# Plain column order for the moving operand of the first twelve feed-forward tasks, and a strided sigmoid read

## The chip, the cores and the metric

The kernel runs on one core of one Trainium2 chip. The metric is device microseconds (us) of one execution, lower is better. The engines are TensorE (PE, with its weight loads as PEld), VectorE (DVE), ScalarE (ACT), GpSimd (POOL) and SyncE (SP). SP and POOL issue nearly all the DMAs here.

## The reference, cut to what matters

Per batch and head a recurrent state of 48 by 48 is decayed, updated and read at each of 768 steps. The 3072 output rows of width 384 then go through a feed-forward network (FFN). With `x` the reshaped output of the recurrence:

```python
y[:, :, t] = einsum('bhd,bhde->bhe', rt, state + cur)
state = wt[:, :, :, None] * state + einsum('bhd,bhe->bhde', kt, vt)
h = x @ w_in                                  # 3072x384 by 384x2048
g = h * (1.0 / (1.0 + np.exp(-1.702 * h)))
out = g @ w_out                               # 2048x384
```

## The kernel before, in words

The 3072 tokens are cut into 24 chunks of 128, and the chunks into six groups of four. `chunk` (L232) computes one chunk of the recurrence in steps on TensorE, VectorE and ScalarE, and leaves it as a high and a low part in fp32r in the tile `x` of its group (128 partitions, 512 token columns). The last twelve chunks (`CROSS`, L75) keep their heads in swapped halves; this touches no line of the change.

The FFN has 96 tasks: six groups by 16 slices of 128 hidden columns. A task has three parts.

- `first_product` (L433) fills the PSUM bank `ph` (two buffers) by nine matmuls of 128 by 512, three terms (high by high, high by low, low by high) for each of three slices of the contraction: L440, L441, L442.
- `gelu` (L445) runs the sigmoid form of gelu twice from `ph` on ScalarE, into `gh` (fp32r, L451) and `gf` (fp32, L452), and VectorE takes the difference as `gl` (L453).
- `second_product` (L456) adds nine matmuls into the three PSUM banks `po`: L466, L467, L468.

The moving operand of each of these matmuls is read through `halves` (L425): column 0, column 256, column 1, column 257 and so on, so two columns that follow each other in the stream lie 1,024 bytes apart. The result is written in memory order (`by_twos`, L429, only gives the output the same shape). Each product thus permutes its columns once. After two products the tokens lie four apart, and `store` (L561) puts them right: its activation L567 reads `po` with a step of four elements (16 bytes) and writes in order.

The weights come as 64-bit integers, and `convert` (L187) turns each of twelve pieces of 128 by 1024 into two fp32r tiles (`pair`). Its six long instructions are L195 and L196 on ScalarE, L198 and L201 on VectorE, then L204 (ScalarE) and L206 (VectorE). The views `l` and `h` (L192) are every second 32-bit word, so L195 (reads and writes `l`), L196 (reads `h`), L198 (reads `h` and `l`, writes `h`) and L201 (reads `h`) step 8 bytes from element to element. L204 and L206 read and write in order.

The order of all work on every engine is written out by hand. Up to task 31 it is the string `RAMP` (L60): `a` is a step of a chunk, `l` a load, `w` a step of a weight conversion, `f` a fetch, `k` a run of bf16 matmuls without use that keeps TensorE busy (L481), and `g`, `h`, `y` with a number are the first product, the gelu and the second product of that task. Tasks 0 to 11 lie where the weights are still being converted. From task 32 on nearly all FFN matmuls run in halves of 64 rows (`on_rows`, L489, matmul L492), two at a time; the last task runs on full rows again. The branch behind L698 (a slower path for extreme inputs) is not entered.

Of the kernel before, what the change touches and what calls it, by code (L numbers as in the profile page):

```python
# [13 lines left out]
AF = mybir.ActivationFunctionType  # L14
# [12 lines left out]
C = P  # L27
# [3 lines left out]
NF = DFF // P  # L31
NM = DM // P
# [8 lines left out]
W_SCALE = 2.0 ** 8  # L41
# [34 lines left out]
WP = NF * DM // NL  # L76
SPLIT = range(FIRST, len(TASKS) - 1)
PHASE = 8
SYNC = mybir.DependencyInfo(mybir.DependencyClass.Sync, mybir.DependencyReason.DATA)
assert sum(CHUNKS) == NT  # L80

# [2 lines left out]
def rwkv_ffn_kernel(ctx: ExitStack, tc, wkr, vp, vrk, ub, w_in, w_out, masks, vt, uc, out):  # L84
    nc = tc.nc
    V, A, G, T = nc.vector, nc.scalar, nc.gpsimd, nc.tensor
# [82 lines left out]
    def fetch(i):  # L169

        s, which = divmod(i, 2)
        n = SL // NL
        st = staged[i] = wt.tile([P, n, 2 * WP // n], I32, tag=f"w{i}", name=f"raw{i}")
        src = (w_in, w_out)[which][s * n : (s + 1) * n].bitcast(I32)
        if which == 0:
            if s == 0:
                nc.sync.dma_start(st[TOP:], src[:, 0 : P - TOP].rearrange("n p w -> p n w"))
            else:
                rows = w_in.bitcast(I32).rearrange("s p w -> (s p) w")[s * n * P - TOP : (s + 1) * n * P - TOP]
                nc.sync.dma_start(st, rows.rearrange("(n p) w -> p n w", p=P))  # L180
            yield
            nc.sync.dma_start(st[0:TOP], src[:, P - TOP :].rearrange("n p w -> p n w"))
        else:
            nc.sync.dma_start(st, src.rearrange("n p w -> p n w"))
        yield
# [23 lines left out]
    def weight(which, f, m):  # L209

        s, n = divmod(f * NM + m, WP // P)
        return (pairs[2 * s + which][:, t, n * P : (n + 1) * P] for t in range(2))

    def split(hi, lo, f):
        A.copy(hi, f)
        V.tensor_tensor(lo, f, hi.bitcast(F32), op=ALU.subtract)  # L216
# [196 lines left out]
    def fill_x(x, c0, c1, cross=False):  # L413

        for m in range(NM):
            for i, dst in enumerate((R2, 0)):
                j = TOP * (2 * m + i + 1)
                G.dma_start(  # L418
                    x[dst : dst + TOP, :, m ^ 2 * (cross and i == 0), c0:c1].bitcast(F32),
                    x[j : j + TOP, :, NM ^ 2 * (cross and j >= HB), c0:c1].bitcast(F32),  # L420
                )

    xs, po, parts, measures, tiled, steady = {}, {}, {}, {}, [], []

    def halves(x):  # L425

        return x.rearrange("p (a b) -> p b a", a=2)

    def by_twos(x):  # L429

        return x.rearrange("p (b a) -> p b a", a=2)

    def first_product(j, task):  # L433
        i, c0, c1, f = task
        cs = slice(c0 * C, c1 * C)
        ph = ps_h.tile([P, WIDE], F32, tag="ph", name="ph")[:, 0 : (c1 - c0) * C]
        x = xs.get((i, 0), xs[i])
        for c in range(NM):
            h_, l_ = weight(0, f, c)
            T.matmul(by_twos(ph), h_, halves(x[:, 0, c, cs]), start=c == 0, stop=False)  # L440
            T.matmul(by_twos(ph), h_, halves(x[:, 1, c, cs]), start=False, stop=False)  # L441
            T.matmul(by_twos(ph), l_, halves(x[:, 0, c, cs]), start=False, stop=c == NM - 1)  # L442
        parts[j] = ph

    def gelu(j, task):  # L445
        i, c0, c1, f = task
        ph, n = parts[j], (c1 - c0) * C
        gf = mo.tile([P, WIDE], F32, tag="gf", name="gf")[:, 0:n]
        gh = mo.tile([P, WIDE], F32R, tag="gh", name="gh", bufs=LAG + 1)[:, 0:n]
        gl = mo.tile([P, WIDE], F32R, tag="gl", name="gl", bufs=LAG + 1)[:, 0:n]  # L450
        A.activation(gh, ph, AF.Gelu_apprx_sigmoid, scale=1.0 / W_SCALE)  # L451
        A.activation(gf, ph, AF.Gelu_apprx_sigmoid, scale=1.0 / W_SCALE)  # L452
        V.tensor_tensor(gl, gf, gh.bitcast(F32), op=ALU.subtract)  # L453
        parts[j] = gh, gl

    def second_product(j, task):  # L456
        i, c0, c1, f = task
        gh, gl = parts.pop(j)
        first = i not in po
        if first:  # L460
            po[i] = [ps_o.tile([P, WIDE], F32, tag=f"po{m}", name=f"po{m}") for m in range(NM)]
        for m in range(NM):
            h_, l_ = weight(1, f, m)
            o = by_twos(po[i][m][:, c0 * C : c1 * C])

            T.matmul(o, h_, halves(gh), start=first, stop=False, skip_group_check=True)  # L466
            T.matmul(o, l_, halves(gh), start=False, stop=False, skip_group_check=True)  # L467
            T.matmul(o, h_, halves(gl), start=False, stop=f == NF - 1, skip_group_check=True)  # L468

    idle = []  # L470

# [17 lines left out]
    def on_rows(half, bank, out, w, x, start, stop, done):  # L489
# [4 lines left out]
        if before:  # L494
            tc.add_manual_dep(mm.ins, before, SYNC, reason="the bank's other row tile is done")
        if done:
            nop = nc.sync.nop()  # L497
            tc.add_manual_dep(nop.ins, mm.ins.name, SYNC, reason="a row tile is done with a bank")
            relay[bank] = nop.ins.name
# [39 lines left out]
    def rows_of(j):  # L539
# [11 lines left out]
        for k in range(2 * n):  # L551
            for items in (top, bottom):
                if k < len(items) and items[k]:
                    next(items[k], None)
            if k == PHASE and j in SPLIT:
                yield
# [19 lines left out]
    def new_x(i):  # L576

        return mo.tile([P, 2, NP, WIDE], F32R, tag="x", name="x")
# [119 lines left out]
    with tc.If(n < full):  # L698
        with tc.tile_pool(name="wp", bufs=2) as wp:
            for i in range(2 * NL):  # L700
                for part in (fetch(i), convert(i, wp, True)):
                    for _ in part:
                        pass
        with tc.tile_pool(name="gp", bufs=1) as gp, tc.tile_pool(name="ob", bufs=2) as ob, tc.For_i(0, B, 1) as b:
            pools["late"] = ob
            xg = [new_x(i) for i in range(2)]
            for p in range(NP):
                vr = gp.tile([R2, S], F32, tag="vr", name="vr")
                V.memset(vr[0:TOP], 0.0)
                nc.sync.dma_start(vr[TOP:R2], vt[bass.ds(b, 1), p].rearrange("o r s -> (o r) s"))  # L710
                uu = gp.tile([R2, D], F32, tag="uu", name="uu")
                V.memset(uu[0:TOP], 0.0)
                nc.sync.dma_start(uu[TOP:R2], uc[p])
                ya = gp.tile([R2, S], F32, tag="ya", name="ya")
                for d in range(D):
                    rows = []
                    for i, c0 in enumerate((1 + p * CW, 1 + NP * CW + p * C, 1 + NP * CW + NP * C + p * C)):
                        x = gp.tile([R2, CB, C], F32, tag=f"row{i}", name=f"row{i}", bufs=2)
                        for h, n in enumerate((HB, D)):
                            src = wkr[bass.ds(b * CB, CB), h * D + d, c0 : c0 + C]  # L720
                            nc.sync.dma_start(x[h * HB : h * HB + n], src.unsqueeze(0).broadcast_to([n, CB, C]))
                        rows.append(x.rearrange("r c s -> r (c s)"))
                    w_, k_, r_ = rows
                    kv = gp.tile([R2, S], F32, tag="kv", name="kv", bufs=2)
                    V.tensor_tensor(kv, k_, vr, op=ALU.mult)
                    st = gp.tile([R2, S + 1], F32, tag="st", name="st", bufs=2)
                    V.memset(st[:, 0:1], 0.0)
                    V.tensor_tensor_scan(st[:, 1:], w_, kv, 0.0, op0=ALU.mult, op1=ALU.add)
                    V.scalar_tensor_tensor(kv, kv, uu[:, d : d + 1], st[:, 0:S], op0=ALU.mult, op1=ALU.add)
                    if d == 0:  # L730
                        V.tensor_tensor(ya, kv, r_, op=ALU.mult)
                    else:
                        V.tensor_tensor(kv, kv, r_, op=ALU.mult)
                        V.tensor_tensor(ya, ya, kv, op=ALU.add)
                for half in range(2):
                    x = xg[half]
                    split(x[0:R2, 0, p, 0:384], x[0:R2, 1, p, 0:384], ya[:, half * 384 : half * 384 + 384])
                    if p == NM:
                        fill_x(x, 0, 384)
            for half in range(2):  # L740
                xs[half] = xg[half]
                for f in range(NF):
                    task = half, 0, 3, f
                    first_product(f, task)
                    gelu(f, task)
                    second_product(f, task)
                store(half, b * S + half * 384, 384)


# [52 lines left out]
```

## Time and profile before

| what | value |
|---|---|
| median of 3 runs | 517.76 us (517.01 to 518.64) |
| the profiled execution | 517.63 us |
| span of its profile | 515.9 us |
| TensorE busy | 495.0 us, 96% of the span |
| VectorE busy | 295.5 us, 57% |
| ScalarE busy | 289.8 us, 56% |
| mean granted TensorE clock | 0.993 |

The span runs from the first to the last recorded instruction; 1.7 us of the execution's time lie around it. A matmul's busy time includes its pipeline, so matmuls that follow each other without a gap overlap in the records, and the distance from start to start is what one costs. The shares over the whole span hide that the first 160 us have other limits than the rest.

### The profile page before, as it was taken

Reading aid. Unit: us, or ns where it says so; the run is one execution under the profiler, and the core shown is the slowest. Engines: PE = TensorE matmul, PEld = TensorE weight load, DVE = VectorE, ACT = ScalarE, POOL = GpSimd, SP = SyncE. Lnnn points to the kernel's source line nnn. Section 1 sums busy time; section 2 is a strip of 40 time slices with the busy share of each in tenths; the row PEclk is TensorE's granted clock in tenths of the full one; section 3 lists DMA queues with packets and bytes.
Section 4 is the critical chain, followed back from the end, with each engine's and each line's share of the span. In section 5 each row is a group of like instructions: output and inputs, shape, how many; then the busy total and the mean of one; then the engine's idle time right before and its main releaser. Section 6 shows DMA issues by size and latency. Waiting matters only on the chain.

```text
span 515.9 us, 11452 instructions
## 1 busy us (share of the span) xinstructions
PE 495.0 (96%) x4539; PEld 417.4 (81%) x4539; DVE 295.5 (57%) x451; ACT 289.8 (56%) x619; POOL 95.8 (19%) x200
## 2 busy tenths in 40 slices
PE   7999988999998999999999999999999999999994
PEld 4766776888886888878888888898888888888873
DVE  7999999999968312645555554564565422211210
ACT  4988989977864443355455475455365342422322
POOL 2002000000200010048401649301660002210000
PEclk9999999999999999989999999999999999999998
DMA  8998920124463210025210435110531001150001
GB/s 270 302 407 232 352 96 1 63 88 148 134 209 96 82 31 0 1 87 141 67 48 12 114 95 159 42 47 6 120 109 47 1 1 32 44 143 1 1 1 68
DMA packets 19470, 50.30 MB, mean 98 GB/s; under 512 B 4544, under 2 KB 8320, under 8 KB 19408
## 3 DMA queue, kind: packets, MB, share of 16 engines
q1 hardware_dynamic: 11664, 31.24, 18.4%
q0 software_dynamic: 7344, 17.72, 13.2%
q8 instruction: 38, 0.62, 0.5%
q10 hardware_dynamic: 400, 0.53, 0.3%
q14 instruction: 24, 0.20, 0.1%
HBM read 40.82 MB, written 4.72 MB: 88 GB/s over the span
## 4 chain that ended last, share of the span: by engine, by line
PE 68%; DVE 1%; DMA 1%; ACT 0%; SPq 0%; issue 0%; ACTq 0%
PE po L492 26%; PE ph L492 24%; PE ps_s L352 3%; PE ps_c L370 2%; PE po L468 2%; PE po L466 2%; PE ph L440 2%; PE po L467 2%; PE ph L441 2%; PE ph L442 2%; PE ps_c L364 1%; PE ps_u L325 1%; DMA rk_t<-in_vrk 1%; PE ps_t L294 0%; PE ps_y L392 0%; PE ps_y L400 0%
## 5 line engine op out<-in xcount | busy, mean ns | idle before, releaser
L492 PE MATMUL ph<-x,pair 64*128 64x512 f32 x1134 | 186.1, 377 | 0.0
L453 DVE TENSOR_TENSOR gl<-gf,gh 128x512 fp32r<-128x512 f32 x96 | 66.3, 691 | 187.1 <-ACT gf L452 187.0
L492 PE MATMUL po<-gh,pair 64*128 64x512 f32 x768 | 159.0, 388 | 0.2 <-SPq L497 0.2
L492 PEld LDWEIGHTS ph<-x,pair 64*128 64x128 f32 x1134 | 144.0, 187 | 14.1
L451 ACT ACTIVATE gh<-ph 128x512 fp32r<-128x512 f32 x96 | 57.5, 599 | 160.2 <-PE ph L492 137.1
L492 PEld LDWEIGHTS po<-gh,pair 64*128 64x128 f32 x768 | 96.2, 188 | 10.9 <-issue 1.1
L492 PE MATMUL po<-gl,pair 64*128 64x512 f32 x384 | 99.8, 379 | 0.0
L418 POOL DMA_DIRECT2D x<-x x36 | 18.3, 514 | 255.2 <-DVE x L216 214.0
L314 ACT ACTIVATE am<-ident,s 128x128 f32<-128x128 f32 x192 | 58.8, 397 | 2.5 <-issue 1.5
L452 ACT ACTIVATE gf<-ph 128x512 f32<-128x512 f32 x96 | 57.1, 595 | 0.0
L157 POOL DMA_DIRECT2D wkr_t<-in_wkr x108 | 53.9, 506 | 11.4 <-DVE kq L266 6.2
L492 PEld LDWEIGHTS po<-gl,pair 64*128 64x128 f32 x384 | 50.5, 188 | 5.0
L440 PE MATMUL ph<-x,pair 128*128 128x512 f32 x99 | 39.0, 393 | 3.7 <-ACT gf L452 2.8
L468 PE MATMUL po<-gl,pair 128*128 128x512 f32 x96 | 36.8, 383 | 3.4 <-DVE gl L453 3.4
L442 PE MATMUL ph<-x,pair 128*128 128x512 f32 x99 | 37.6, 380 | 0.0
L441 PE MATMUL ph<-x,pair 128*128 128x512 f32 x99 | 37.5, 379 | 0.0
L466 PE MATMUL po<-gh,pair 128*128 128x512 f32 x96 | 37.3, 389 | 0.0
L467 PE MATMUL po<-gh,pair 128*128 128x512 f32 x96 | 36.4, 380 | 0.0
L221 ACT ACTIVATE junk<-lp 112x1032 bf16<-112x1032 f32 x24 | 25.9, 1077 | 12.0 <-DVE lp L251 11.9
L245 DVE TENSOR_TENSOR_SCAN lp<-wkr_t,d1r 112x516 f32<-112x516 f32 x24 | 29.5, 1228 | 1.3 <-POOL ident masks.py:199 0.9
L251 DVE TENSOR_TENSOR_SCAN lp<-wkr_t,d1f 112x516 f32<-112x516 f32 x24 | 29.4, 1225 | 0.1
L355 DVE COPY_PREDICATED am<-after,ps_s 128x512 f32<-128x512 int32 x40 | 26.9, 727 | 0.2
(90 smaller groups left out, 642.6 us busy)
## 6 DMA issues: line engine op xcount, KB each, us to landing
wkr_t<-in_wkr SPq DMA_DIRECT2D x10, 770.5 KB, 4.7
raw<-in_w_out SPq DMA_DIRECT2D x6, 1024.0 KB, 11.2
raw<-in_w_in SPq DMA_DIRECT2D x5, 1024.0 KB, 12.2
wkr_t<-in_wkr POOLq DMA_DIRECT2D x72, 48.0 KB, 2.1
rk_t<-in_vrk POOLq DMA_DIRECT2D x9, 384.0 KB, 3.6
out_t<-ob POOLq DMA_DIRECT2D x12, 256.0 KB, 2.6
v_t<-in_vrk SPq DMA_DIRECT2D x15, 192.0 KB, 4.3
rk_t<-in_vrk SPq DMA_DIRECT2D x7, 384.0 KB, 4.0
```

Of the source, the lines that this page charges most:

```text
L157: queue[0].dma_start(a[dst : dst + D, cols], wkr[t, src : src + D, cols])
L314: A.activation(x_[:, p], ident, AF.Copy, scale=s[:, j : j + 1])
L440: T.matmul(by_twos(ph), h_, halves(x[:, 0, c, cs]), start=c == 0, stop=False)
L441: T.matmul(by_twos(ph), h_, halves(x[:, 1, c, cs]), start=False, stop=False)
L442: T.matmul(by_twos(ph), l_, halves(x[:, 0, c, cs]), start=False, stop=c == NM - 1)
L451: A.activation(gh, ph, AF.Gelu_apprx_sigmoid, scale=1.0 / W_SCALE)
L452: A.activation(gf, ph, AF.Gelu_apprx_sigmoid, scale=1.0 / W_SCALE)
L453: V.tensor_tensor(gl, gf, gh.bitcast(F32), op=ALU.subtract)
L466: T.matmul(o, h_, halves(gh), start=first, stop=False, skip_group_check=True)
L467: T.matmul(o, l_, halves(gh), start=False, stop=False, skip_group_check=True)
L468: T.matmul(o, h_, halves(gl), start=False, stop=f == NF - 1, skip_group_check=True)
L492: mm = T.matmul(by_twos(out), w[rows], halves(x[rows]), start=start, stop=stop, skip_group_check=True)
```

## The change

Tasks with a number below `PLAIN` (12) read `x`, `gh` and `gl` in memory order, and their outputs keep that order. So that `po` gets the same token order as from all other tasks, their two activations read `ph` with an inner step of 128 elements (512 bytes): four columns 128 apart, then the next four, and write `gh` and `gf` in order. Nothing else differs: the same instructions in the same order, with other access patterns in 216 matmuls (12 tasks by 18) and 24 activations. In the branch that is not entered the task numbers are raised by 16 so that it stays as it was.

```diff
+PLAIN = 12
...
-    def halves(x):
-
-        return x.rearrange("p (a b) -> p b a", a=2)
+    def halves(x, plain=False):
+
+        return x if plain else x.rearrange("p (a b) -> p b a", a=2)
...
+    def by_fours(x):
+
+        return x.rearrange("p (c b) -> p b c", c=4)
...
+        plain = j < PLAIN
...
+        o = by_twos(ph, plain)
...
-            T.matmul(by_twos(ph), h_, halves(x[:, 0, c, cs]), start=c == 0, stop=False)
...
+            T.matmul(o, h_, halves(x[:, 0, c, cs], plain), start=c == 0, stop=False)
...
-        A.activation(gh, ph, AF.Gelu_apprx_sigmoid, scale=1.0 / W_SCALE)
-        A.activation(gf, ph, AF.Gelu_apprx_sigmoid, scale=1.0 / W_SCALE)
+        for g in (gh, gf):
+            if j < PLAIN:
+                A.activation(
+                    g.rearrange("p (b c) -> p b c", c=4), by_fours(ph), AF.Gelu_apprx_sigmoid, scale=1.0 / W_SCALE
+                )
+            else:
+                A.activation(g, ph, AF.Gelu_apprx_sigmoid, scale=1.0 / W_SCALE)
...
-            T.matmul(o, h_, halves(gh), start=first, stop=False, skip_group_check=True)
...
+            T.matmul(o, h_, halves(gh, plain), start=first, stop=False, skip_group_check=True)
...
-                    first_product(f, task)
-                    gelu(f, task)
-                    second_product(f, task)
+                    first_product(f + NF, task)
+                    gelu(f + NF, task)
+                    second_product(f + NF, task)
```

## Rows read from the trace of the kernel before

**Rows 1.** The page: busy time, share and instructions of each engine.

```profile
PE 495.0 (96%) x4539; PEld 417.4 (81%) x4539; DVE 295.5 (57%) x451; ACT 289.8 (56%) x619; POOL 95.8 (19%) x200
```

**Rows 2.** Busy time by stage; columns as in the first line.

```profile
core 0: us, PE busy (x) PEld busy (x) DVE busy (x) ACT busy (x) POOL busy (x), PEclk, DMA share, GB/s
46.80:108.00 61.20, 55.38 (x325) 45.33 (x323) 58.87 (x65) 57.13 (x96) 0.00 (x0) 1.00 0.39 135
108.00:145.00 37.00, 36.36 (x316) 30.89 (x316) 36.21 (x59) 28.92 (x64) 3.00 (x6) 1.00 0.49 151
160.00:515.90 355.90, 347.69 (x3392) 302.04 (x3388) 147.41 (x247) 161.10 (x368) 86.14 (x168) 0.99 0.21 57
```

**Rows 3.** Waits of TensorE, 46 to 165 us: us in total, times, longest.

```profile
PE po L468 <- DVE gl L453: 3.4, 3, 2.0
PE ph L440 <- ACT gf L452: 2.8, 3, 1.7
PE ps_d L274 <- DVE x L216: 0.6, 1, 0.6
PE ps_d L274 <- DVE rku L258: 0.6, 1, 0.6
```

**Rows 4.** Waits of VectorE, 46.8 to 158 us, same columns.

```profile
DVE rk_t L261 <- DMA rk_t<-in_vrk: 3.5, 1, 3.5
DVE gl L453 <- ACT gf L452: 2.1, 4, 0.8
```

**Rows 5.** Groups by line, ScalarE and VectorE, 0 to 46.8 us: busy us, mean ns.

```profile
L196 ACT ACTIVATE c<-raw 128x1024 f32<-128x1024 f32 x3 | 3.5, 1159 | 0.0
L195 ACT ACTIVATE raw<-raw 128x1024 int32<-128x1024 uint32 x3 | 3.5, 1157 | 0.0
L201 DVE SCALAR_TENSOR_TENSOR c<-c,raw 128x1024 int32<-128x1024 int32 x2 | 2.5, 1226 | 0.1
L198 DVE SCALAR_TENSOR_TENSOR raw<-raw 128x1024 int32<-128x1024 int32 x2 | 2.4, 1212 | 0.0
```

**Rows 6.** The same view, 46.8 to 106 us.

```profile
L198 DVE SCALAR_TENSOR_TENSOR raw<-raw 128x1024 int32<-128x1024 int32 x9 | 14.0, 1555 | 0.0
L201 DVE SCALAR_TENSOR_TENSOR c<-c,raw 128x1024 int32<-128x1024 int32 x9 | 13.2, 1470 | 0.3
L206 DVE TENSOR_TENSOR pair<-c,pair 128x1024 fp32r<-128x1024 f32 x9 | 10.9, 1219 | 0.0
L196 ACT ACTIVATE c<-raw 128x1024 f32<-128x1024 f32 x9 | 13.4, 1489 | 0.8 <-DVE pair L206 0.8
L195 ACT ACTIVATE raw<-raw 128x1024 int32<-128x1024 uint32 x8 | 11.9, 1487 | 0.0
```

**Rows 7.** Timeline of ScalarE: start us, us, what.

```profile
79.59 1.16 ACT L196 ACTIVATE c<-raw 128x1024 f32<-128x1024 f32 x1
...
83.12 1.64 ACT L196 ACTIVATE c<-raw 128x1024 f32<-128x1024 f32 x1
```

**Rows 8.** Timeline of TensorE, the same columns.

```profile
79.39 1.05 PE L400 MATMUL ps_y<-kq,sf 112*48 112x128 f32 x16
...
84.56 0.38 PE L466 MATMUL po<-gh,pair 128*128 128x512 f32 x1
84.77 0.38 PE L467 MATMUL po<-gh,pair 128*128 128x512 f32 x1
```

**Rows 9.** Timeline of TensorE: bf16 matmuls that read 512 columns in memory order.

```profile
39.55 3.20 PE L481 MATMUL idle<-d1r 112*128 112x512 bf16 x14
```

**Rows 10.** Groups by line over the whole span: two ScalarE reads of PSUM.

```profile
L451 ACT ACTIVATE gh<-ph 128x512 fp32r<-128x512 f32 x96 | 57.5, 599 | 160.2 <-PE ph L492 137.1 <-PE ph L442 20.3 <-PE po L467 2.8
L567 ACT ACTIVATE ob<-po 128x512 f32<-128x512 f32 x18 | 9.8, 597 | 4.8 <-PE po L492 2.4 <-PE po L468 2.3
```

**Rows 11.** Timeline of SP's DMA issues.

```profile
143.47 5.50 SPq L157 DMA_DIRECT2D wkr_t<-in_wkr  x12
```

**Rows 12.** Busy time in one stretch, columns as in rows 2.

```profile
220.00:230.00 10.00, 9.29 (x91) 7.96 (x93) 4.30 (x8) 6.79 (x18) 3.74 (x8) 0.83 0.26 88
```

More of the change, by code (lines that the diff above doesn't have):

```diff
@@ L423, in rwkv_ffn_kernel, with by_twos @@
     xs, po, parts, measures, tiled, steady = {}, {}, {}, {}, [], []
-    def halves(x):
-        return x.rearrange("p (a b) -> p b a", a=2)
-    def by_twos(x):
-        return x.rearrange("p (b a) -> p b a", a=2)
+    def halves(x, plain=False):
+        return x if plain else x.rearrange("p (a b) -> p b a", a=2)
+    def by_twos(x, plain=False):
+        return x if plain else x.rearrange("p (b a) -> p b a", a=2)
+    def by_fours(x):
+        return x.rearrange("p (c b) -> p b c", c=4)
     def first_product(j, task):
@@ L439, in first_product @@
             h_, l_ = weight(0, f, c)
-            T.matmul(by_twos(ph), h_, halves(x[:, 0, c, cs]), start=c == 0, stop=False)
-            T.matmul(by_twos(ph), h_, halves(x[:, 1, c, cs]), start=False, stop=False)
-            T.matmul(by_twos(ph), l_, halves(x[:, 0, c, cs]), start=False, stop=c == NM - 1)
+            T.matmul(o, h_, halves(x[:, 0, c, cs], plain), start=c == 0, stop=False)
+            T.matmul(o, h_, halves(x[:, 1, c, cs], plain), start=False, stop=False)
+            T.matmul(o, l_, halves(x[:, 0, c, cs], plain), start=False, stop=c == NM - 1)
         parts[j] = ph
@@ L463, in second_product @@
             h_, l_ = weight(1, f, m)
-            o = by_twos(po[i][m][:, c0 * C : c1 * C])
-            T.matmul(o, h_, halves(gh), start=first, stop=False, skip_group_check=True)
-            T.matmul(o, l_, halves(gh), start=False, stop=False, skip_group_check=True)
-            T.matmul(o, h_, halves(gl), start=False, stop=f == NF - 1, skip_group_check=True)
+            plain = j < PLAIN
+            o = by_twos(po[i][m][:, c0 * C : c1 * C], plain)
+            T.matmul(o, h_, halves(gh, plain), start=first, stop=False, skip_group_check=True)
+            T.matmul(o, l_, halves(gh, plain), start=False, stop=False, skip_group_check=True)
+            T.matmul(o, h_, halves(gl, plain), start=False, stop=f == NF - 1, skip_group_check=True)
     idle = []
```

## The prediction

> **What bounds the kernel now.** I read the page first: TensorE is busy 96% of the span [rows 1]. That is an average over stages, so the view by stage comes next [rows 2]. After 160 us TensorE is busy 347.7 of 355.9 us and everything else less than half of that: there it is the limit, and the change touches nothing there. Tasks 0 to 11 lie between 46.8 us (the first FFN matmul) and about 120 us, and most of them in 46.8 to 108. In that stage VectorE is busy 58.9 of 61.2 us and ScalarE 57.1, both more than TensorE (55.4). The waits say the same from the other side: up to 108.8 us TensorE waits 2.8 us for `gf` (ScalarE holds back one of the two `ph` banks), 1.4 us for `gl` (3.4 less the one wait of 2.0, which lies at 157.6), and 0.6 + 0.6 us for VectorE's chunk work, 5.4 us in all [rows 3]. So the ramp belongs to VectorE and ScalarE, and what is saved or lost on them there moves the start of a long TensorE-bound stretch.
>
> Then I looked for instructions that take longer in this stage than elsewhere. Before the first FFN matmul the four conversion instructions with 8-byte steps take 1157 (L195), 1159 (L196), 1212 (L198) and 1226 ns (L201) [rows 5]. In 46.8 to 106 us the same four average 1487, 1489, 1555 and 1470 ns, while L206, of the same size but in memory order, takes 1219 [rows 6]. The timeline tells when. L196 takes 1.16 us at 79.59 beside fp32 matmuls that read in memory order (L400, then L352), and 1.64 us at 83.12 beside the FFN matmuls that read in halves [rows 7, 8]. I read the others against TensorE's timeline in the same way: of the 38 that run after 46.8 us, each one that lies wholly beside FFN matmuls is long, and each beside other matmuls is within 40 ns of its early value. So steps of 8 bytes on ScalarE and VectorE are slowed while TensorE streams interleaved columns.
>
> **The change part by part.**
>
> TensorE, 216 matmuls: two that follow each other start 0.21 us apart (84.56, 84.77) while they read interleaved [rows 8]. The bf16 matmuls that read 512 columns in memory order take the same: 14 in 3.20 us; less the 0.38 us of the last, 13 distances of 0.217 [rows 9]. Reading in memory order cannot go below that row, so I take 0 for TensorE itself. From the other side, a slower plain read of fp32r is not shown by any row; L400 streams fp32 in memory order, 16 records of 128 columns in 1.05 us, without sign of it [rows 8].
>
> Conversions: if reading in memory order frees the stepped accesses, VectorE saves 9 x (1555 - 1212) = 3.1 us at L198 and 9 x (1470 - 1226) = 2.2 us at L201, together 5.3. ScalarE saves 8 x (1487 - 1157) = 2.6 us at L195 and 9 x (1489 - 1159) = 3.0 us at L196, together 5.6 [rows 5, 6]. The lower bound is no saving at all: no row shows fp32r streamed in memory order. I take nearly the whole, because the nearest rows (L400 in fp32, L481 in bf16, both plain) leave the stepped instructions at their short times.
>
> [...]
>
> Activations, 24 of them: from reading `ph` in order (599 ns) to an inner step of 512 bytes. The nearest row is L567, a read of PSUM with a step of 16 bytes: 597 ns, no cost [rows 10]. The far bound is the stretch that ScalarE shows on stepped reads of SBUF under load, 1489 to 1159, or 28%: 0.17 us each, 4.1 us in all. I take 0. What hides a small surplus is ScalarE's slack, 61.2 - 57.1 = 4.1 us in the stage, plus the 5.6 saved; what waits behind a longer gelu is the next first product, which needs the `ph` bank, and VectorE's `gl`.
>
> DMAs, waits and instruction order stay as they are; no semaphore is added.
>
> **Sum.** Three things limit how far the end of the ramp moves: what VectorE saves (5.3), what ScalarE saves (5.6), and the waits that TensorE can lose (5.4). They agree within 0.3 us. From 108 to 145 us TensorE (36.4 of 37.0) and VectorE (36.2) are both full [rows 2], so neither can win more there, and both carry the lead along. The last place where it could be lost is the wait of 3.5 us for `rk_t` before 153.8 us [rows 4]: that DMA stands on SP's queue behind twelve chunk loads that take 5.5 us to issue from 143.5 on [rows 11], and those follow VectorE's chunk work and the first store, so they come earlier by the same lead. TensorE's wait of 2.0 us at 157.6 is late next, and stays. I take off 0.3 us from the smallest term because two long conversions after 106 us meet matmuls of tasks 12 and up, which stay interleaved, and earlier work can slide beside them. That makes 5.0 us: 517.63 - 5.0 = 512.6. The profiled execution (517.63, its span 515.9 and 1.7 around it) stands 0.13 us below the median of the runs, so no correction is made.
>
> [...]
>
> **The rivals.**
>
> 1. The order makes no difference to the neighbours: fp32r at the full column rate crowds stepped accesses in either order. For it: every slow row lies beside fp32r, and no plain fp32r row exists. Against it: the plain bf16 and fp32 streams disturb nothing. Then nothing is saved, 517.6. Chance 0.17. [...]
>
> 2. Half of it goes: the accesses collide less but still do, or a new wait for `gf` takes back half. 517.63 - 2.6 = 515.0. Chance 0.13.
>
> 3. Slower: ScalarE's read with 512-byte steps is expensive. Its place is L451 and L452 of tasks 0 to 11, each TensorE wait for `gf` grows. It decides from (5.6 + 4.1) / 24 = 0.40 us more for each activation, when the saving and the slack are used up. At twice the time, 24 x 0.6 = 14.4 us, the surplus is 14.4 - 9.7 = 4.7: 522.3. Against it: L567 at 597 ns. For it: four neighbours 512 bytes apart is a step that no row has. Chance 0.11. [...]
>
> 4. Plain fp32r columns stream more slowly on TensorE. 216 matmuls at, say, 10% more cost 216 x 0.022 = 4.7 us, most of it beside waits that exist; only far more than that makes the kernel slower. At half rate it would be 216 x 0.216 = 46.7 us, over 550. No row points to it. Chance 0.04.
>
> That the change does not do what it says is hardly possible: the patterns are in the instructions, and only the values' order in `ph` changes.
>
> **How the numbers follow.** The forecast has 0.55 and its own range is 510.2 to 514.2: below, 5.3 plus the 2.1 us that VectorE waits for `gf` [rows 4] from 517.63; above, the clock's 1.7 lost once more. With rivals 1 and 2 it makes 0.85, so the range goes up to 518.6, the highest run shown. A measurement of this kernel can tell about 0.3% (1.6 us) from no change. Faster by more than that: forecast and rival 2, 0.68. Same: rival 1, 0.17. Slower: rivals 3 and 4, 0.15.
>
> **What would show it.** In the profile after: L195 and L196 at about 1160 ns, L198 at 1212 and L201 at 1226 in the stage of tasks 0 to 11, except beside tasks from 12 on; L451 and L452 of those tasks still near 600 ns; FFN matmuls 0.216 us apart; TensorE's waits for `gf` and `gl` before 108 us gone or nearly so; the first matmul of half rows, at 212 us before, about 5 us earlier, and the rest of the span unchanged. The prediction is wrong if the conversions stay near 1490 to 1550 ns, if L451 grows past 0.9 us, or if the lead seen at 108 us is no longer there at 160.

## The result, and the profile after

The changed kernel takes 511.56 us (median of 4 runs, 511.18 to 512.61) against 517.6 us of the kernel before: ratio 0.9884, 95% interval 0.9862 to 0.9907. It is 6.0 us faster, where 5.0 were forecast. The profiled execution takes 511.32 us, its span 509.6.

Line numbers move by 1 to 13 in the changed kernel: L195, L196, L198, L201 and L206 are now L196, L197, L199, L202 and L207; L451 and L452 are one line, L460, for tasks 0 to 11 and L464 for the others; L453, which writes `gl`, is L465; L440 to L442 are L447 to L449, L466 to L468 are L479 to L481, and the half-row matmul L492 is L505.

First the conversions and the activations: groups by line of the changed kernel, 46.8 to 106 us, in the columns of [rows 6].

```profile
L202 DVE SCALAR_TENSOR_TENSOR c<-c,raw 128x1024 int32<-128x1024 int32 x9 | 11.0, 1226 | 0.3
L199 DVE SCALAR_TENSOR_TENSOR raw<-raw 128x1024 int32<-128x1024 int32 x9 | 11.0, 1220 | 0.4 <-ACT c L197 0.4
L196 ACT ACTIVATE raw<-raw 128x1024 int32<-128x1024 uint32 x10 | 11.7, 1174 | 0.6 <-DMA raw<-in_w_in 0.6
L197 ACT ACTIVATE c<-raw 128x1024 f32<-128x1024 f32 x9 | 10.4, 1154 | 1.0 <-DVE pair L207 1.0
L460 ACT ACTIVATE gh<-ph 128x512 fp32r<-128x512 f32 x12 | 7.2, 600 | 0.4 <-PE ph L449 0.4
L460 ACT ACTIVATE gf<-ph 128x512 f32<-128x512 f32 x12 | 7.2, 602 | 0.0
```

All four conversion lines are back within 17 ns of their times from before the first FFN matmul [rows 5], and the activations with the 512-byte step take what L451 took in order [rows 10]. The last piece is converted after 105 us, where matmuls of tasks 12 and up, which stay interleaved, run again from 106.0 to 110 us. The timelines of ScalarE and VectorE:

```profile
105.12 1.26 ACT L196 ACTIVATE raw<-raw 128x1024 int32<-128x1024 uint32 x1
106.17 1.64 ACT L197 ACTIVATE c<-raw 128x1024 f32<-128x1024 f32 x1
107.93 1.70 DVE L199 SCALAR_TENSOR_TENSOR raw<-raw 128x1024 int32<-128x1024 int32 x1
```

L197 and L199, which lie wholly beside them, are long: L197 takes what L196 took at 83.12 us before [rows 7]. L196 at 105.12 us lies mostly beside small matmuls and is nearly short.

TensorE's waits, 40 to 165 us, in the columns of [rows 3]:

```profile
PE po L481 <- DVE gl L465: 1.8, 1, 1.8
PE ph L447 <- DMA x<-x: 1.2, 1, 1.2
PE ps_t L301 <- DVE kq L267: 0.4, 1, 0.4
PE ps_d L275 <- DVE rku L259: 0.3, 1, 0.3
```

The waits for `gf` are gone, and of those for `gl` the one is left that was expected to stay. From 47.2 to 103 us, in the stage of tasks 0 to 11, TensorE, VectorE and ScalarE are now busy nearly alike (columns as in [rows 2]):

```profile
47.20:103.00 55.80, 54.56 (x321) 45.01 (x320) 53.68 (x64) 52.40 (x97) 0.00 (x0) 1.00 0.44 148
```

What I had not expected stands in TensorE's timeline, start us and duration:

```profile
53.16 0.39 PE L448 MATMUL ph<-x,pair 128*128 128x512 f32 x1
53.39 0.39 PE L449 MATMUL ph<-x,pair 128*128 128x512 f32 x1
53.61 0.39 PE L447 MATMUL ph<-x,pair 128*128 128x512 f32 x1
...
54.75 0.39 PE L449 MATMUL ph<-x,pair 128*128 128x512 f32 x1
```

From 53.16 to 54.75 us there are seven distances: 0.227 us each, where the interleaved order had 0.216 [rows 8]. A plain fp32r matmul costs 11.5 ns more (227.1 against 215.6 before rounding), 216 of them 2.5 us.

Where the 6 us come from is read at two marks. The first matmul on half rows starts at 212.29 us before and at 207.95 after:

```profile
212.29 1.11 PE L492 MATMUL ph<-x,pair 64*128 64x512 f32 x4
```

```profile
207.95 1.11 PE L505 MATMUL ph<-x,pair 64*128 64x512 f32 x4
```

So 4.3 us are won up to there. From there to the last half-row matmul it takes 290.4 us before (502.67 - 212.29) and 288.7 after (496.63 - 207.95). The instructions are the same; the 1.7 us are the clock. (The two profiled executions differ by 6.3 us; the last 0.3 lie behind that matmul.) Busy time by stretch, first before, then after, columns as in [rows 2]:

```profile
222.00:226.00 4.00, 4.00 (x22) 3.25 (x24) 1.94 (x3) 2.43 (x8) 0.46 (x1) 0.57 0.01 4
```

```profile
217.00:222.00 5.00, 5.00 (x62) 4.44 (x63) 1.95 (x3) 4.81 (x13) 1.80 (x4) 1.00 0.16 55
```

Before, the granted clock is 0.50 for 3.4 us behind the thin stretch of small matmuls, from 222.1 to 225.5 us; the mean of 0.57 over 4 us is a loss of 0.43 x 4 = 1.7. After, the same place stays at 1.00. The thin stretch itself is the same in both: TensorE is idle for 1.1 us of 212.29 to 222 us before, and of 207.95 to 217 us after.

### The profile page after: what moved, and what is told of

The parts are those of the page before. It is cut to its first block, busy times and chain, and to the rows that moved or that the text cites. A ratio compares the mean times of both kernels' runs of the same rounds, so it can differ in the third digit from the quotient of the medians.

```text
span 509.6 us, 11452 instructions
## 1 busy us (share of the span) xinstructions
PE 493.9 (97%) x4539; PEld 416.5 (82%) x4539; DVE 290.6 (57%) x451; ACT 285.0 (56%) x619; POOL 95.5 (19%) x200
## 4 chain that ended last, share of the span: by engine, by line
PE 68%; DVE 1%; DMA 1%; ACT 0%; SPq 0%; issue 0%; ACTq 0%
PE po L505 26%; PE ph L505 24%; PE ps_s L353 3%; PE ps_c L371 2%; PE po L481 2%; PE po L479 2%; PE ph L447 2%; PE po L480 2%; PE ph L449 2%; PE ph L448 2%; PE ps_c L365 1%; PE ps_u L326 1%; DMA rk_t<-in_vrk 1%; PE ps_t L295 0%; PE ps_y L393 0%; PE ps_y L401 0%
## 5 line engine op out<-in xcount | busy, mean ns | idle before, releaser
L505 PE MATMUL ph<-x,pair 64*128 64x512 f32 x1134 | 185.5, 376 | 0.0
L465 DVE TENSOR_TENSOR gl<-gf,gh 128x512 fp32r<-128x512 f32 x96 | 66.3, 690 | 184.3 <-ACT gf L464 183.6
L505 PE MATMUL po<-gh,pair 64*128 64x512 f32 x768 | 157.8, 385 | 0.2 <-SPq L510 0.2
L505 PEld LDWEIGHTS ph<-x,pair 64*128 64x128 f32 x1134 | 143.4, 186 | 14.0
L464 ACT ACTIVATE gh<-ph 128x512 fp32r<-128x512 f32 x84 | 50.1, 597 | 160.7 <-PE ph L505 137.2
L505 PEld LDWEIGHTS po<-gh,pair 64*128 64x128 f32 x768 | 95.5, 186 | 10.7 <-issue 1.1
L505 PE MATMUL po<-gl,pair 64*128 64x512 f32 x384 | 99.2, 376 | 0.0
L505 PEld LDWEIGHTS po<-gl,pair 64*128 64x128 f32 x384 | 50.0, 186 | 4.8
L464 ACT ACTIVATE gf<-ph 128x512 f32<-128x512 f32 x84 | 49.8, 593 | 0.0
L447 PE MATMUL ph<-x,pair 128*128 128x512 f32 x99 | 39.0, 394 | 1.2 <-DMA x<-x 1.2
L481 PE MATMUL po<-gl,pair 128*128 128x512 f32 x96 | 36.9, 384 | 1.8 <-DVE gl L465 1.8
L449 PE MATMUL ph<-x,pair 128*128 128x512 f32 x99 | 37.9, 383 | 0.0
L479 PE MATMUL po<-gh,pair 128*128 128x512 f32 x96 | 37.7, 393 | 0.0
L222 ACT ACTIVATE junk<-lp 112x1032 bf16<-112x1032 f32 x24 | 25.7, 1069 | 11.5 <-DVE lp L252 11.4
L246 DVE TENSOR_TENSOR_SCAN lp<-wkr_t,d1r 112x516 f32<-112x516 f32 x24 | 29.4, 1226 | 1.4 <-DMA wkr_t<-in_wkr 1.0
L252 DVE TENSOR_TENSOR_SCAN lp<-wkr_t,d1f 112x516 f32<-112x516 f32 x24 | 29.4, 1225 | 0.1
## 6 DMA issues: line engine op xcount, KB each, us to landing
raw<-in_w_out SPq DMA_DIRECT2D x6, 1024.0 KB, 11.5
```

Source lines behind the costliest of these rows:

```text
L246: V.tensor_tensor_scan(li.rearrange("r p c -> r (p c)")[:, ::-1], w1[:, ::-1], d1r.rearrange("r p c -> r (p c)")[:, ::-1], 0.0, op0=ALU.mu ...
L447: T.matmul(o, h_, halves(x[:, 0, c, cs], plain), start=c == 0, stop=False)
L449: T.matmul(o, l_, halves(x[:, 0, c, cs], plain), start=False, stop=c == NM - 1)
L464: A.activation(g, ph, AF.Gelu_apprx_sigmoid, scale=1.0 / W_SCALE)
L479: T.matmul(o, h_, halves(gh, plain), start=first, stop=False, skip_group_check=True)
L481: T.matmul(o, h_, halves(gl, plain), start=False, stop=f == NF - 1, skip_group_check=True)
```

## The experiments

Each kernel is compared with the kernel before on the same chip. Three questions were open after the result: whether the order of the matmuls alone makes the gain, what in an order the neighbours and TensorE pay for, and how much of the gain is the clock.

**The activations alone.** Of the changed kernel only the stepped read in `gelu` is kept.

```diff
-        plain = j < PLAIN
+        plain = False
...
-            plain = j < PLAIN
+            plain = False
```

> One part of the change alone: in tasks 0 to 11 only the two activations read with the 512-byte step, all matmuls read in halves as before the change; the tokens of the first group come out in another order. Theory (the gain comes from the order of the matmuls alone, and the stepped read is free): activations at 600 to 615 ns, conversions at 1470 to 1560 ns, time as the kernel before within 0.3%, 515.5 to 518. Rival (the stepped read itself shortens or lengthens something): off by more than 1.6 us either way.

Measured: 516.81 us against 517.76, ratio 0.999 (0.9971 to 1.0009). Groups by line, 46.8 to 106 us:

```profile
L199 DVE SCALAR_TENSOR_TENSOR raw<-raw 128x1024 int32<-128x1024 int32 x9 | 14.2, 1580 | 0.0
L460 ACT ACTIVATE gh<-ph 128x512 fp32r<-128x512 f32 x11 | 6.6, 598 | 0.0
```

The stepped read costs nothing and brings nothing. The conversions are long again. The gain belongs to the matmuls' order.

**Half of the matmuls.** Only first products read plain; the gelu then applies one permutation instead of two.

```diff
-            plain = j < PLAIN
+            plain = False
             o = by_twos(po[i][m][:, c0 * C : c1 * C], plain)
...
-        return x.rearrange("p (c b) -> p b c", c=4)
+        return x.rearrange("p (c b) -> p b c", c=2)
...
-                    g.rearrange("p (b c) -> p b c", c=4), by_fours(ph), AF.Gelu_apprx_sigmoid, scale=1.0 / W_SCALE
+                    g.rearrange("p (b c) -> p b c", c=2), by_fours(ph), AF.Gelu_apprx_sigmoid, scale=1.0 / W_SCALE
```

> The changed kernel with only the first products of tasks 0 to 11 in plain order; their second products read in halves as before the change, and the gelu reads with an inner step of 1,024 bytes, two columns at a time. Theory (each stepped conversion pays while an interleaved matmul runs beside it, in proportion): conversions beside first products are short, beside second products long, means about half way (1320, 1320, 1385, 1350 ns); VectorE saves half of 5.3 us and TensorE pays half of 2.5, so 517.6 - 2.6 to 517.6 - 3.5, 514 to 515. Rival (only one of the two, x or gh, shares something with the weights' buffers): all of the gain or none of it, 511 or 517.5.

Measured: 514.2 us against 516.82, ratio 0.9951 (0.9924 to 0.9977). The four means are 1346, 1282, 1362 and 1275 ns; the shortest of L199 in that stage is 1218, the longest 1714. Half of the plain matmuls bring part of the relief and 2.6 us. The rival, all or nothing, is out.

This run also shows the cause within one profile. VectorE's timeline, then where first products (L447) and second products (L479) begin on TensorE:

```profile
57.38 1.23 DVE L199 SCALAR_TENSOR_TENSOR raw<-raw 128x1024 int32<-128x1024 int32 x1
59.78 1.71 DVE L199 SCALAR_TENSOR_TENSOR raw<-raw 128x1024 int32<-128x1024 int32 x1
```

```profile
57.40 0.40 PE L447 MATMUL ph<-x,pair 128*128 128x512 f32 x1
59.46 0.38 PE L479 MATMUL po<-gh,pair 128*128 128x512 f32 x1
```

The first L199 lies beside plain first products and is short; the second, 2.4 us later, lies beside interleaved second products and is long. The other conversions of the stage go the same way: those wholly beside first products take 1.16 to 1.23 us, those wholly beside second products 1.52 us or more.

**More plain matmuls than there are conversions.**

```diff
-PLAIN = 12
+PLAIN = 32
```

The second products of tasks 30 and 31 run in the half-row code and stay interleaved there, so that two slices are added in another column order.

> The changed kernel with plain order up to task 31 instead of task 11. Theory (plain order costs TensorE 11.5 ns in each matmul, and frees only stepped conversions, of which only four are left after task 11): 20 more tasks of 18 matmuls, 360 x 0.0115 = 4.1 us more on TensorE, which is full from 110 us on; the two long conversions after 105 us become short (L197 1637 to 1160, L199 1696 to 1220, together 1.0 us) with little use. So 511.6 + 3 to 511.6 + 4.1: 514.6 to 515.7. Rival (the longer plain matmul is hidden by waits as it seems to be in the ramp, or comes only beside the weight DMAs): 511 to 512.

Measured: 514.39 us against 516.82, ratio 0.9955 (0.9932 to 0.9979). The median is 2.8 us above that of the changed kernel in its first comparison. Each counted from the kernel before beside it, 2.4 us are left of the 6.0, so 3.6 are lost. Expected were 3 to 4.1. The last conversions became short, as expected:

```profile
104.83 1.14 ACT L197 ACTIVATE c<-raw 128x1024 f32<-128x1024 f32 x1
106.43 1.22 DVE L199 SCALAR_TENSOR_TENSOR raw<-raw 128x1024 int32<-128x1024 int32 x1
```

The timeline has plain matmuls 0.227 us apart far from any weight DMA:

```profile
147.05 0.39 PE L447 MATMUL ph<-x,pair 128*128 128x512 f32 x1
147.28 0.39 PE L448 MATMUL ph<-x,pair 128*128 128x512 f32 x1
147.50 0.39 PE L449 MATMUL ph<-x,pair 128*128 128x512 f32 x1
```

So the 11.5 ns belong to the plain order and not to the ramp's traffic, and where TensorE is full (37.0 of 37.0 us in 108 to 145) they show in the time.

**What in the order matters: coarser blocks.** The interleave of all tasks takes four columns at a time from each half. In this run and those below, `by_twos` changes along with `halves`, so that outputs are still written in memory order; those lines are left out.

```diff
-        return x.rearrange("p (a b) -> p b a", a=2)
+        return x.rearrange("p (a b k) -> p b a k", a=2, k=4)
...
-                ob.rearrange("p (c b) -> p c b", c=4), o[:, 0:N].rearrange("p (b c) -> p c b", c=4),
+                ob.rearrange("p (c b k) -> p c b k", c=4, k=4), o[:, 0:N].rearrange("p (b c k) -> p c b k", c=4, k=4),
```

> The kernel before, with the interleave of all tasks made coarser: every moving operand is read as four columns of the one half, four of the other (16 bytes at a time), the gelu reads in order everywhere and the store unpicks the order. [...] Theory C (two streams far apart crowd the neighbours whatever their grain): conversions stay near 1490 to 1550 ns and the time stays at 517.6.

Measured: 570.01 us, ratio 1.1039 (1.099 to 1.1087). Timeline of TensorE, then one group of 46.8 to 106 us:

```profile
85.25 0.41 PE L440 MATMUL ph<-x,pair 128*128 128x512 f32 x1
85.49 0.42 PE L441 MATMUL ph<-x,pair 128*128 128x512 f32 x1
85.75 0.41 PE L442 MATMUL ph<-x,pair 128*128 128x512 f32 x1
```

```profile
L198 DVE SCALAR_TENSOR_TENSOR raw<-raw 128x1024 int32<-128x1024 int32 x9 | 14.6, 1617 | 0.0
```

Theory C fails in the time: matmuls are 0.25 us apart, slower than in either order (0.216 and 0.227). The conversions are long, as it expected: L198 takes 1617 ns, where the old order had 1555 [rows 6]. For the neighbours C stands: two places far apart, whatever the grain.

**One rising stream with a step.** Tasks 0 to 11 read every fourth column, in four passes. Theory C is that of the run above: the neighbours pay for two streams far apart.

```diff
-        return x if plain else x.rearrange("p (a b) -> p b a", a=2)
+        return x.rearrange("p (b a) -> p a b", a=4) if plain else x.rearrange("p (a b) -> p b a", a=2)
```

> The changed kernel, with tasks 0 to 11 reading their moving columns in one rising stream with a step of 16 bytes (every fourth column, four passes), the gelu and all else as in the changed kernel; the tokens of the first group come out in another order. [...] Theory C (two distant streams are what they pay for): conversions at 1160 to 1226 ns and about 511.5 us. [...]

Measured: 561.83 us, ratio 1.0868 (1.0819 to 1.0917). Timeline, then a group of 46.8 to 106 us:

```profile
57.94 0.64 PE L447 MATMUL ph<-x,pair 128*128 128x512 f32 x1
58.40 0.64 PE L448 MATMUL ph<-x,pair 128*128 128x512 f32 x1
58.86 0.64 PE L449 MATMUL ph<-x,pair 128*128 128x512 f32 x1
```

```profile
L199 DVE SCALAR_TENSOR_TENSOR raw<-raw 128x1024 int32<-128x1024 int32 x7 | 8.5, 1220 | 0.0
```

A matmul takes 0.46 us, twice the plain one, which I had not expected. The neighbours are left alone, L199 at 1220 ns, as theory C expected: here the step of 16 bytes hurts TensorE and not them. By this run alone they could also be spared because TensorE reads at half the rate. The pairs of 16 bytes below settle that: at 0.216 us a matmul L199 takes 1222 ns.

**Pairs at other distances.** Tasks 0 to 11 alternate at every column, as before the change, between places 16, 64, 128 or 256 bytes apart (k = 4, 16, 32, 64).

```diff
-        return x if plain else x.rearrange("p (a b) -> p b a", a=2)
+        return x.rearrange("p (b a k) -> p b k a", a=2, k=4) if plain else x.rearrange("p (a b) -> p b a", a=2)
```

> The changed kernel, with tasks 0 to 11 alternating at every column as before the change, but between places 16 bytes apart instead of 1,024 (columns 0, 4, 1, 5, 2, 6, 3, 7, then the next eight); gelu and all else as in the changed kernel, so that the tokens of the first group come out in another order. [...] Theory E (what makes TensorE faster is what the neighbours pay for, at any distance): 0.216 us and conversions at 1490 to 1550 ns, time as before the change. Theory F (TensorE's gain itself needs two distant places): 0.227 us or more, conversions short, time as the changed kernel or slower.

> The same with places 256 bytes apart (columns 0, 64, 1, 65 and so on in blocks of 128). [...] Theory E: 0.216 us and 1490 to 1550 ns. Theory F: if this distance is enough for TensorE, as in theory E, else as the plain order.

> Tasks 0 to 11 alternate between places 64 bytes apart (columns 0, 16, 1, 17 and so on); token order of the first group as in the runs with 16 and 256 bytes. It places the step between 16 bytes (conversions short) and 256 bytes (conversions long). [...]

> Tasks 0 to 11 alternate between places 128 bytes apart; token order of the first group as in the other runs with pairs. At 64 bytes the conversions were short (1181, 1214, 1220 and 1227 ns), at 256 long (1505, 1511, 1568 and 1464). Whatever tells near from far, the means lie at one of the two levels, not between: near 1160 to 1230 if the border is between 128 and 256, near 1470 to 1570 if it is between 64 and 128. Matmuls 0.216 us apart.

Measured: 513.85 us at 16 bytes (ratio 0.9929, 0.9896 to 0.9962), 516.64 at 256 (0.9989, 0.9966 to 1.0012), and in single runs 510.11 at 64 and 511.18 at 128. Timeline at 16 bytes:

```profile
57.20 0.38 PE L449 MATMUL ph<-x,pair 128*128 128x512 f32 x1
57.41 0.38 PE L447 MATMUL ph<-x,pair 128*128 128x512 f32 x1
57.63 0.38 PE L448 MATMUL ph<-x,pair 128*128 128x512 f32 x1
```

One group of 46.8 to 106 us at 16, 64, 128 and 256 bytes, a fence for each:

```profile
L199 DVE SCALAR_TENSOR_TENSOR raw<-raw 128x1024 int32<-128x1024 int32 x9 | 11.0, 1222 | 0.0
```

```profile
L199 DVE SCALAR_TENSOR_TENSOR raw<-raw 128x1024 int32<-128x1024 int32 x9 | 11.0, 1220 | 0.0
```

```profile
L199 DVE SCALAR_TENSOR_TENSOR raw<-raw 128x1024 int32<-128x1024 int32 x9 | 11.0, 1225 | 0.0
```

```profile
L199 DVE SCALAR_TENSOR_TENSOR raw<-raw 128x1024 int32<-128x1024 int32 x9 | 14.1, 1568 | 0.0
```

Matmuls are 0.216 us apart at every distance, so theory F is out. L199 takes 1225 ns at 128 bytes and 1568 at 256, so the border for the neighbours lies between the two, and theory E, in which they pay at any distance, is out. TensorE's 2.5 us did not show in the time. At 16 bytes the three runs with a mean clock of 0.996 or 0.997 take 510.2 to 510.8 us, no less than the changed kernel, and the other six, with 0.986 to 0.994, take 512.8 to 516.5. TensorE is quicker, but it waits again: 0.8 us for `gf` and 2.2 for `gl` where the changed kernel has none and 1.8:

```profile
PE po L481 <- DVE gl L465: 2.2, 1, 2.2
...
PE ph L447 <- ACT gf L460: 0.8, 1, 0.8
```

After the wait of 2.2 us this profile has a drop of the clock, too (a mean of 0.66 in 153 to 158 us). So nearly all of the 2.5 us that plain order costs TensorE is hidden: VectorE's and ScalarE's chain sets the pace. How much is left can be estimated from the traces. From the first FFN matmul to the 216th, less the wait for the DMA that fills `x` in between (0.5 to 2.2 us), the changed kernel takes 59.4 us in both of its profiles, and the kernels with pairs of 16, 64 and 128 bytes take 58.9 to 59.0: TensorE's 2.5 us are worth about 0.4.

**A kernel to beat both.** The pairs of 16 bytes in all tasks, from the kernel before.

```diff
-        return x.rearrange("p (a b) -> p b a", a=2)
+        return x.rearrange("p (b a k) -> p b k a", a=2, k=4)
...
-                ob.rearrange("p (c b) -> p c b", c=4), o[:, 0:N].rearrange("p (b c) -> p c b", c=4),
+                ob.rearrange("p (b x y) -> p b x y", x=4, y=2), o[:, 0:N].rearrange("p (b y x) -> p b x y", x=4, y=2),
```

> The kernel before with its interleave narrowed in all tasks: every moving operand alternates between places 16 bytes apart (columns 0, 4, 1, 5, 2, 6, 3, 7 of each eight), the gelu reads in order everywhere and the store unpicks the order. [...] VectorE limits the ramp, so against the changed kernel at the same granted clock it gains 0 to 1 us: 509.5 to 510.5. Rival: TensorE being quicker than VectorE only waits more, and the clock drops more often, as in the run with 16-byte pairs in tasks 0 to 11: median 511.5 to 514.

Measured: 510.74 us against 516.25, ratio 0.9894 (0.9866 to 0.9922). It beats the kernel before, and cannot be told from the changed kernel (0.9884 and 0.9872 in its two comparisons); the forecast was 509.5 to 510.5. All conversions are short, also the four after 105 us (1.14 to 1.22 us). The half-row stretch takes 288.7 us, as in the profile after: narrow pairs change nothing there.

**The clock's share.** The changed kernel again. In the two profiles above 4.3 us lie ahead of the half rows, and 1.7 us are the drop of the clock near 222 us, which only the profile of before has.

> The changed kernel once more, unchanged, beside the kernel before, for how much of the difference is the granted clock. [...] Theory (the clock's drop is chance and comes to both kernels): runs of the two kernels with the same mean clock differ by about 4.3 us, and the medians by 4.3 to 5.3. Rival (the change itself removes the drop): the changed kernel's runs nearly all show a mean clock of 0.997, those of before 0.993 to 0.994, and the medians differ by 6.

Measured: 510.36 us against 517.25, ratio 0.9872 (0.9847 to 0.9896). All five runs have a mean clock of 0.997 or 0.998. Of the 20 runs of before beside them ten have 0.993 or 0.994 and a median of 517.7, the other ten 0.996 or more and 516.2. At equal clock the difference is thus 5.9 us, more than the 4.3 expected from the first pair of profiles, and the medians differ by 6.9, more than the 4.3 to 5.3 of the theory. Of the rival's forecast the part on the changed kernel came true, and of the runs of before only half are at 0.993 or 0.994. In this second profile the half rows begin at 206.80 us, 5.5 earlier than before.

```profile
206.80 0.89 PE L505 MATMUL ph<-x,pair 64*128 64x512 f32 x3
```

Whether the change makes the drop rarer stays open. Over the comparisons of the experiments 31 of 63 runs of before have a mean clock under 0.995, and one of nine of the changed kernel. The other kernels lean to the rival: with all conversions short it is two of ten (plain up to task 31) and one of six (narrow pairs in all tasks), with long or half-long ones six of ten (the activations alone), six of ten (256 bytes) and five of ten (half of the matmuls). Against it stand six of nine with pairs of 16 bytes in tasks 0 to 11, whose profile has its drop in another place. No run was made to separate the two.

## Why the prediction was right, step by step

- **The stage.** That VectorE and ScalarE set the ramp's pace held. Most directly, the runs with narrow pairs gave TensorE back its 2.5 us and won about 0.4 in the ramp.
- **The conversions.** VectorE was to save 5.3 us: 9 x (1555 - 1220) + 9 x (1470 - 1226) = 5.2. ScalarE's lines fell to 1174 and 1154 ns as forecast. The bound from the nearest rows, plain bf16 and fp32, came true, although no row showed plain fp32r. That was partly luck: the same step from other formats to fp32r failed for TensorE, below.
- **The neighbours' dependence on the order.** L195 takes 1487 ns before and, as L196, 1174 after, by the order in which TensorE reads, with GpSimd at 0.00 us busy in the stage both times. Rival 1 is out.
- **The activations.** 0 was right: 600 against 599 ns. L567, whose step of 16 bytes cost nothing (597 ns [rows 10]), told it; rival 3 is out.
- **TensorE at 0: the term that was wrong.** I said that reading in memory order costs TensorE nothing, since bf16 does not (0.217 us a matmul [rows 9]) and L400 showed no sign. It costs 2.5 us. Rival 4 had the mechanism, at half of the 10% that I set there as an example, and was right that waits would cover it. The price of its half rate, 46.7 us, is near what the 16-byte step cost: 45.0 us at 0.460 us a matmul. Rows of another number format were not enough for this term.
- **The sum.** 5.0 us was 0.7 too much for the first profile's mark at the half rows (4.3) and 0.5 too little for the second (5.5). The ramp itself gave the same in both. TensorE's timeline at the first and the 216th FFN matmul, before, then in the two profiles of the changed kernel:

```profile
46.82 0.48 PE L440 MATMUL ph<-x,pair 128*128 128x512 f32 x1
112.66 0.38 PE L442 MATMUL ph<-x,pair 128*128 128x512 f32 x1
```

```profile
47.19 0.50 PE L447 MATMUL ph<-x,pair 128*128 128x512 f32 x1
107.83 0.38 PE L449 MATMUL ph<-x,pair 128*128 128x512 f32 x1
```

```profile
46.74 0.50 PE L447 MATMUL ph<-x,pair 128*128 128x512 f32 x1
107.33 0.38 PE L449 MATMUL ph<-x,pair 128*128 128x512 f32 x1
```

  That is 65.8 us before, and 60.6 after both times: 5.2 us, what VectorE was to save. The rest lies around the ramp: in the first profile it starts 0.4 us late and the way from there to the half rows is 0.5 us longer than before, in the second it starts 0.1 early and that way is 0.2 shorter.
- **The waits TensorE can lose.** This limit was put at 5.4 us and was too small. 198 of these 216 matmuls read plain, which costs 2.3 us, and still the ramp is 5.2 shorter, so about 7.5 us of delay went. [rows 3] holds only the longer waits; short gaps between matmuls went too: before, the matmul behind the one at 55.70 us starts 0.45 us later, and after the change the same distance is 0.22. That 7.5 less 2.3 comes out beside the 5.4 is luck: two terms were off and cancel.
- **The clock.** The measured 6.0 has up to 1.7 more from the clock, which I had put into the range only (its upper end, 512.6 + 1.7, is 514.3, not 514.2). No row shows these 1.7 us: [rows 12] has a mean clock of 0.83 in 10 us and not the level it fell to. The profiles showed 0.50 for 3.4 us, and 290.4 against 288.7 us for the same half rows.

## What to carry to other kernels

An access order is not only a matter for the engine that reads: here TensorE's moved VectorE's L198 from 1555 to 1220 ns. Where instructions of the same shape have two durations, look at what another engine reads at that time, and in which order. Before an engine is made quicker, look for whom it waits: in this ramp 5% on each matmul were worth about 0.4 us of 2.5, and from task 12 on the same 5% cost 3 to 4 us.

## What the runs showed that I had not expected

The order in which TensorE reads 512 fp32r columns from SBUF sets two costs that have little to do with each other: TensorE's own, and that of ScalarE and VectorE when they step by 8 bytes at the same time.

| order of the moving columns | us between matmuls | L198/L199 beside it, ns |
|---|---|---|
| rising, 4 bytes | 0.227 | 1220 |
| rising, 16 bytes | 0.460 | 1220 |
| alternating at each column, 16, 64, 128 bytes apart | 0.216 | 1222, 1220, 1225 |
| alternating at each column, 256 bytes apart | 0.216 | 1568 |
| alternating at each column, 1,024 bytes apart | 0.216 | 1555 |
| alternating every four columns, 1,024 bytes apart | 0.25 | 1617 |

In TensorE's own cost the rising stream with a 16-byte step is the slowest, 0.460 us, and alternating at every column the quickest, 0.216 us; what sets it, no run here shows. Nor does any show why the neighbours pay at 256 and 1,024 bytes (1568 and 1555 ns) and not up to 128 (1225). All the distances that were run are powers of two, and 512 was not run, so the distance cannot be told from the address bit in which the two places differ.
